# Three transposing loads for the first 512 rows of a cross network, in place of TensorE transposes

## The chip, the cores and the metric

The kernel runs on one core of one Trainium2 chip. The metric is device time in microseconds (us), the median of several runs. One execution is also taken with the hardware profiler; its span runs from the first instruction to the last. The engines are TensorE (PE; its weight loads are listed apart as PEld), VectorE (DVE), ScalarE (ACT), GpSimd (POOL) and SyncE (SP). DMAs are issued by SP and by ACT, each from its own queue of instructions.

## The reference

Six cross layers over 4096 rows of 416 features, in bf16. Each layer is a 416 x 416 matmul, a bias, a product with the input `x0`, and a sum with the layer's own input.

```python
B, F, D, L = 4096, 26, 16, 6
Din = min(F * D, 1024)          # 416
x0: (B, Din)   ws: (L, Din, Din)   bs: (L, Din)

def reference(x0, ws, bs):
    x = x0
    for l in range(ws.shape[0]):
        x = x0 * (x @ ws[l] + bs[l]) + x
    return x
```

## The kernel before

**The algebra.** Since `x` is always `x0` times something, the kernel never adds `x` back. It lets PSUM keep the sum of all layers' products: after layer l the banks hold the sum of `x_i @ W_i` for i up to l, and `x_{l+1} = x0 * (sum + summed biases + 1)`. The biases are summed once by a small matmul (`bias_sums`), with a row of ones for the 1.

**The tiling.** Rows are taken in 4 blocks of 1024 (`s`), each in two halves of 512 (`h`). The 416 features are 3 chunks of 128 (`c`, `m`, `k`) and a tail of 32. Activations are held transposed, features on partitions: `x0T_sb` has the 3 chunks of all rows, `xT_sb` the current layer's. The tail has its own layout: four groups of 256 rows are stacked on 128 partitions (`x0t_sb`, `xt_sb`), with a second copy in which neighbouring groups are swapped.

**One layer** (`s`, `l`) in the order in which TensorE gets it:

- `main` for half 0: 3 x 3 groups of four matmuls (128 rows of weights x 32 columns each, 512 moving columns), 36 in all;
- `tail_rows`: the tail's contribution to the chunks (needs `wt_sb`, the last 32 rows of the weights) and, in its second part, the tail's contribution to the tail (needs `wc_sb`, which POOL fills from `wt_sb` by four partition-shifting copies, `corner`);
- `tail_outs`: the chunks' contribution to the tail, for all 1024 rows, so it needs both halves;
- `main` for half 1, another 36 matmuls.

DVE takes each finished bank and multiplies by `x0T_sb` (`leave`, three for each half). ACT and POOL do the same for the tail (`leave_tail`): two ACT operations add the bias, POOL multiplies, and two copies each on ACT and POOL make the swapped copy. In the last layer of the last block the roles of the operands are turned, so that the output comes out by rows; it is not touched by the change.

**The head.** For the first 512 rows there is a special path. Two loads (`load_rows`, one on SP, one on ACT) bring them by rows into `xin_sb`. TensorE transposes them, 128 x 128 at a time, 12 in all, against the identity `ident`; DVE (chunks 0 and 2) and ACT (chunk 1) copy the results from PSUM to `x0T_sb`. Ahead of that TensorE runs 10 filler matmuls on a tile of ones, and 2 more between the two groups of transposes (`fill`). Rows 512 to 1023, and each later block, come by a transposing DMA (`load_transposed`). Layer 0 of block 0 has its own order: `main` goes chunk by chunk (`k` outermost), with `bias_sums` after chunk 0 and the tail's own transposes (`tail_in`, from `xin_sb` for rows 0 to 511 and `xtl_sb` for rows 512 to 1023) after chunk 1, then `tail_outs`, then `tail_rows`.

**What sets the order.** `Plan.add` records every operation by engine with what it reads and writes, and `emit` turns that into semaphore waits. Each engine works through its own list in the order in which the operations were added, and so do the two DMA-issuing queues. The order is thus that of the calls in the source: the loads (L208 to L225), the constants (L228 to L246), the head (L475 to L503), `corner` (L525, L526 and L558) and the loop (L527 on).

The loads, in the order of issue: SP has rows 0 to 255, W0, two of the four pieces of layer 0's tail weights (`wt0`), narrow rows (`xtl0`, 4 groups of 128 rows by 32 columns), the transposing load of rows 512 to 1023, four pieces of `wt1`, W1, four pieces of `wt2` (layers 2 to 5), W2, the other narrow rows, W3 to W5, and three transposing loads of 1024 rows. ACT has rows 256 to 511, the biases, and the other two pieces of `wt0`; its activation table is loaded behind these.

Of the kernel before, what the change touches and what calls it, by code (L numbers as in the profile page):

```python
# [5 lines left out]
BF16 = mybir.dt.bfloat16  # L6
FP32 = mybir.dt.float32
ALU = mybir.AluOpType
ACTF = mybir.ActivationFunctionType
# [109 lines left out]
def bass_standalone__dcn_v2_cross__recsys_kernel(  # L119
# [6 lines left out]
    B, D = x0.shape  # L126
# [15 lines left out]
    with ExitStack() as es:  # L142

        def sb(name, shape, dt=BF16):
            return es.enter_context(nc.sbuf_tensor(name, shape, dt))
# [1 line left out]
        w_sb = sb("w_sb", [128, L, NC, D])  # L147
        wt_sb = sb("wt_sb", [128, L, D])
        wc_sb = sb("wc_sb", [128, L, 2, 128])
        xin_sb = sb("xin_sb", [128, 4, D])  # L150
        xtl_sb = sb("xtl_sb", [128, NJ, DR])
        xr_sb = sb("xr_sb", [128, JS, D])
        x0T_sb = sb("x0T_sb", [128, NC, B])
# [9 lines left out]
        ot_sb = sb("ot_sb", [128, NS - 1, 2, 128])  # L163
        o_sb = sb("o_sb", [128, NJ, D])
        ident = sb("ident", [128, 128])
        ones_sb = sb("ones_sb", [128, 256])
        dummy_sb = sb("dummy_sb", [128, 8])
        bsa_sb = sb("bsa_sb", [L + 1, D])
        u_sb = sb("u_sb", [L + 1, L])
# [3 lines left out]

        x0_v = x0.rearrange("(j p) d -> p j d", p=128)
        out_v = out.rearrange("(j p) d -> p j d", p=128)
        P = Plan()

        def quad(q):
# [6 lines left out]
        def load(queue, dst, src, name, writes):  # L185
            P.add(queue, lambda e: e.dma_start(dst, src), writes=writes, dma=name)

        def load_main(l):
            load(
                "sync", w_sb[:, l, :, :], ws[l, 0:DF, :].rearrange("(k p) n -> p k n", p=128), "w%d" % l, [("w", l)]  # L190
            )

        def load_rows(queue, i):
            load(queue, xin_sb[:, 2 * i:2 * i + 2, :], x0_v[:, 2 * i:2 * i + 2, :], "xin%d" % i, [("xin", i)])

        def load_tail_weights(a, b, name, queues):
            for g in range(4):
# [1 line left out]
                    queues[g], wt_sb[quad(g), a:b, :], ws[a:b, DF:D, :].rearrange("l p n -> p l n"), name, [("wt", name)]  # L199
                )  # L200

        def load_transposed(s, a, b):
            P.add(
                "sync", lambda e: e.dma_start_transpose(x0T_sb[:, :, s * SB + a:s * SB + b], x0[s * SB + a:s * SB + b, 0:DF]),
                writes=[("x0T", s, c, h) for c in CH for h in HALVES if a <= h * H < b], dma="x0T%d" % s,
            )

        load_rows("sync", 0)  # L208
        load_rows("scalar", 1)
        load_main(0)  # L210
        load("scalar", bsa_sb[1:L + 1, :], bs[:, :], "bs", [("bs",)])
        load_tail_weights(0, 1, "wt0", ("sync", "scalar", "sync", "scalar"))
        load("sync", xtl_sb[:, 4:JS, :], x0_v[:, 4:JS, DF:D], "xtl0", [("xtl", 0)])
        load_transposed(0, H, SB)
        load_tail_weights(1, 2, "wt1", ("sync",) * 4)
        load_main(1)
        load_tail_weights(2, L, "wt2", ("sync",) * 4)
        load_main(2)
        load("sync", xtl_sb[:, JS:NJ, :], x0_v[:, JS:NJ, DF:D], "xtl1", [("xtl", 1)])
# [3 lines left out]
        for s in range(1, NS):  # L223
# [3 lines left out]

        P.add("vector", lambda e: e.memset(ones_sb[:, :], 1.0), writes=[("ones",)])  # L228
        P.add(
            "scalar", lambda e: e.activation(out=dummy_sb[:, :], in_=ones_sb[:, 0:8], func=ACTF.Identity, bias=0.0),  # L230
            reads=[("ones",)], writes=[("dummy",)],
        )
        P.add(
            "gpsimd", lambda e: e.affine_select(
# [29 lines left out]
        def fill(n):  # L264
            def fn(pe):
                for i in range(n):
                    ins = pe.matmul(  # L267
                        ps[:, 7, 0:256], lhsT=ones_sb[:, 0:128], rhs=ones_sb[:, :], start=True, stop=True
                    )
                return ins  # L270

            P.add("tensor", fn, reads=[("ones",)], adds=[("ps", 7)])

        def wkey(l):
            return "wt%d" % min(l, 2)
# [85 lines left out]
        def tail_in(s):  # L361
            def fn(pe):
                for o in range(2 if s == 0 else 1):
                    for r in range(2):
                        for g in range(4):
                            j = 2 * (g ^ o) + r
                            src = xin_sb[:, j, DF:D] if s == 0 and j < 4 else xtl_sb[:, s * JS + j, :]
                            b, c = (7, o * G) if s == 0 else (T_BANK[0], G)
                            ins = mm(
                                pe, ps[quad(g), b, c + r * 128:c + (r + 1) * 128], src, ident[:, :],  # L370
                                s == 0 and o == 0 and r == 0, (0, 32 * g),
                            )
                return ins

            b = 7 if s == 0 else T_BANK[0]
            P.add(
                "tensor", fn, reads=[("ident",), ("xtl", 0 if s == 0 else 1)] + ([("xin", 0), ("xin", 1)] if s == 0 else []),
                adds=[("ps", b)],
            )
            if s == 0:  # L380
                P.add(
                    "scalar", lambda e: e.activation(  # L382
                        out=x0t_sb[:, s, :, :], in_=ps[:, 7, :].rearrange("p (o c) -> p o c", o=2), func=ACTF.Copy
                    ), reads=[("ps", 7)], writes=[("x0t", s), ("x0t", s, "swapped")],
                )
# [83 lines left out]
                reads=[("o", s), ("oc", s)], writes=[("out", s)], dma="out%d" % s,  # L469
            )  # L470


        HEAD_BANKS = ((3, 4, 5), (6, 2, 7))
        B_BANK = 6
        fill(10)  # L475
        for i in range(2):
            for c in CH:
                b = HEAD_BANKS[i][c]

                def fn(pe, i=i, c=c, b=b):  # L480
                    for j in range(2):
                        ins = pe.transpose(  # L482
                            out=psT[:, b, j * 128:(j + 1) * 128],
                            in_=xin_sb[:, 2 * i + j, c * 128:(c + 1) * 128], identity=ident[:, :],
                        )
                    return ins

                P.add("tensor", fn, reads=[("xin", i), ("ident",)], adds=[("ps", b)])
                dst, src = x0T_sb[:, c, i * 256:(i + 1) * 256], psT[:, b, 0:256]
                if c == 1:  # L490
                    P.add(
                        "scalar", lambda e, d=dst, s=src: e.activation(out=d, in_=s, func=ACTF.Copy),
                        reads=[("ps", b)], writes=[("x0Tp", c, i)],
                    )
                else:
                    P.add(
                        "vector", lambda e, d=dst, s=src: e.tensor_copy(out=d, in_=s),  # L497
                        reads=[("ps", b)], writes=[("x0Tp", c, i)],
                    )
            if i == 0:  # L500
                fill(2)
        for c in CH:
            P.writer[("x0T", 0, c, 0)] = [w for i in range(2) for w in P.writer[("x0Tp", c, i)]]  # L503

        def bias_sums():
            def fn(pe):
# [16 lines left out]


        corner(0, 1, "wt0")  # L525
        corner(1, 2, "wt1")  # L526
        for s in range(NS):  # L527
            for l in range(L):
                ending = s == NS - 1 and l == L - 2
                if s == NS - 1 and l == L - 1:  # L530
                    break
                if s == 0 and l == 0:
                    for k in CH:
                        for m in CH:
                            main(s, l, 0, m, k)
                        if k == 0:
                            bias_sums()
                        if k == 1:
                            tail_in(0)
                    tail_outs(s, l, True)  # L540
                    tail_rows(s, l, False)
                    for c in CH:
                        leave(s, l, 0, c)
                else:
                    for m in CH:
                        for k in CH:
                            main(s, l, 0, m, k)
                    tail_rows(s, l, l == 0)
                    for c in CH:
                        leave(s, l, 0, c)  # L550
                    tail_outs(s, l, False)
                if l == 2 and s < NS - 1:
                    tail_in(s + 1)
                leave_tail(s, l, not ending)
                if l == 2 and s < NS - 1:
                    keep_tail_in(s + 1)
                if s == 0 and l == 0:
                    corner(2, L, "wt2")  # L558
                if l == 1 and s > 0:
                    store_block(s - 1)  # L560
                if s < NS - 1 and l in (3, 4):
                    g = 2 * (l - 3)
                    swap(x0t_sb[:, s + 1], ("x0t", s + 1), tuple("scalar" if q // 2 == l - 3 else None for q in range(4)))
                if ending:
                    tail_halves(L - 1, st_sb, ("st",))
                    for c in CH:
                        keep_sum(0, c, "scalar")
                for m in CH:
                    for k in CH:
                        main(s, l, 1, m, k)  # L570
                    leave(s, l, 1, m)
                if ending:
                    for c in CH:
                        keep_sum(1, c, ("scalar", "vector", "vector")[c])
            if s < NS - 1:
                transpose_block(s)
# [127 lines left out]
```

## Time and profile before

| | |
|---|---|
| median of 3 runs | 130.66 us (130.54 to 130.81) |
| the profiled execution | 130.68 us, span 129.4 us |
| PE busy | 124.5 us, 96% of the span |
| PEld busy | 64.3 us, 50% |
| DVE busy | 98.9 us, 76% |
| ACT busy | 50.5 us, 39% |
| POOL busy | 38.7 us, 30% |
| HBM read, written | 4.07 MB, 3.41 MB |

"Busy" adds up the time in which an engine has at least one instruction running; matmuls overlap each other, so a busy PE is not PE at its peak. The costliest group is line 259, the matmuls of `mm`, through which nearly all of them go. A row of the timeline reads: start in us from the start of the span, length in us, engine, line of the code, operation, tile written and tile read, shape, and count where neighbours are merged; in brackets the idle time of the engine ahead of it and what ended it. `SPq` and `ACTq` are DMA issues: their length is what the issue takes, not the transfer. The time from issue to landing is listed apart.

### The profile page before, as it was taken

What the parts mean: (1) busy time and instruction counts of PE and PEld (TensorE: products, weight loads), DVE (VectorE), ACT (ScalarE), POOL (GpSimd) and SP (SyncE); (2) the same over time, 40 slices, a digit from 0 to 9 for tenths busy, and PEclk for the clock granted to TensorE, in tenths of its full rate; (3) what the DMA queues carried; (4) which work ended last, traced back from release to release, by engine and by line L of the source; (5) the groups of instructions that cost most, each with busy time, mean ns of one, the idle gap of its engine ahead of it and who ended that gap; (6) DMA issues with size and microseconds to landing.
All of it is one profiled execution on the core that took longest, in us unless ns stands there. A gap on an engine that the chain in (4) does not pass through costs nothing.

```text
span 129.4 us, 5183 instructions
## 1 busy us (share of the span) xinstructions
PE 124.5 (96%) x2352; PEld 64.3 (50%) x2352; DVE 98.9 (76%) x151; ACT 50.5 (39%) x113; POOL 38.7 (30%) x86
## 2 busy tenths in 40 slices
PE   6999999999999999999999999999999999999990
PEld 4544545545545545545545545545545545544650
DVE  0309879779779779788788788798797797797881
ACT  1525225455505224464514233463513243245720
POOL 6044344044024053043123152142122152242050
PEclk9999999999999999999999999999999999999999
DMA  3989999999729307000019208000009507000007
GB/s 111 232 206 223 145 245 213 173 195 170 221 51 156 64 11 262 5 0 5 0 39 193 42 0 268 0 5 0 5 16 132 120 5 263 5 0 5 0 0 263
DMA packets 34065, 13.11 MB, mean 101 GB/s; under 512 B 25334, under 2 KB 34044, under 8 KB 34044
## 3 DMA queue, kind: packets, MB, share of 16 engines
q1 hardware_dynamic: 33248, 12.20, 45.2%
q10 hardware_dynamic: 796, 0.59, 1.4%
q8 instruction: 18, 0.29, 1.0%
q14 instruction: 3, 0.02, 0.1%
HBM read 4.07 MB, written 3.41 MB: 58 GB/s over the span
## 4 chain that ended last, share of the span: by engine, by line
PE 92%; DVE 2%; DMA 2%; ACT 0%; issue 0%
PE ps L259 91%; DVE o_sb L630 2%; DMA xin_sb<-in_x_dram 2%; PE ps L482 1%; ACT x0t_sb L382 0%; PE ps L267 0%
## 5 line engine op out<-in xcount | busy, mean ns | idle before, releaser
L411 DVE SCALAR_TENSOR_TENSOR xT_sb<-ps,cb_sb,x0T_sb 128x512 bf16<-128x512 f32 x120 | 80.9, 743 | 19.8 <-PE ps L259 19.8
L259 PE MATMUL ps<-xT_sb,w_sb 128*32 128x512 bf16 (+1 forms) x1596 | 84.6, 364 | 0.0
L259 PEld LDWEIGHTS ps<-xT_sb,w_sb 128*32 128x32 bf16 x1596 | 40.8, 97 | 37.2 <-issue 4.0
L421 ACT ACTIVATE t_sb<-ps,cb_sb 64x256 f32<-64x256 f32 x46 | 21.6, 470 | 51.1 <-PE ps L259 50.9
L434 POOL TENSOR_TENSOR xt_sb<-t_sb,x0t_sb 128x256 bf16<-128x256 f32 x20 | 13.4, 672 | 63.8 <-ACT t_sb L421 63.8
L398 ACT ACTIVATE xt_sb<-xt_sb 32x256 bf16<-32x256 bf16 x38 | 15.7, 414 | 15.4 <-POOL xt_sb L434 15.2
L259 PE MATMUL ps<-x0T_sb,w_sb 128*32 128x512 bf16 (+1 forms) x336 | 19.5, 373 | 0.1
L400 POOL COPY xt_sb<-xt_sb 32x256 bf16<-32x256 bf16 x38 | 15.0, 394 | 2.4
L411 DVE SCALAR_TENSOR_TENSOR xo_sb<-ps,cb_sb,x0T_sb 128x512 bf16<-128x512 f32 x18 | 12.1, 743 | 2.5 <-PE ps L259 2.5
L259 PEld LDWEIGHTS ps<-x0T_sb,w_sb 128*32 128x32 bf16 x336 | 8.4, 97 | 8.1 <-issue 0.8
L259 PE MATMUL ps<-xt_sb,wt_sb 32*128 32x512 bf16 (+1 forms) x152 | 11.6, 326 | 0.0
L259 PE MATMUL ps<-xt_sb,wc_sb 32*128 32x256 bf16 x76 | 7.3, 268 | 0.0
L259 PEld LDWEIGHTS ps<-xt_sb,wt_sb 32*128 32x128 bf16 x152 | 2.3, 91 | 8.1 <-DVE xT_sb L411 6.4
L259 PE MATMUL ps<-w_sb,xT_sb 128*128 128x416 bf16 x24 | 5.0, 339 | 0.0
L434 POOL TENSOR_TENSOR xot_sb<-t_sb,x0t_sb 128x256 bf16<-128x256 f32 x3 | 2.0, 674 | 9.9 <-ACT t_sb L421 9.9
L398 ACT ACTIVATE x0t_sb<-x0t_sb 32x256 bf16<-32x256 bf16 x12 | 4.9, 410 | 0.1
L252 POOL COPY wc_sb<-wt_sb 32x32 bf16<-32x32 bf16 (+1 forms) x12 | 2.8, 234 | 5.5 <-DMA wt_sb<-in_ws_dram 4.9
L267 PE MATMUL ps<-ones_sb 128*128 128x256 bf16 x12 | 2.9, 419 | 1.3 <-DVE ones_sb L228 1.3
L259 PEld LDWEIGHTS ps<-xt_sb,wc_sb 32*128 32x128 bf16 x76 | 3.9, 93 | 0.3
L497 DVE COPY x0T_sb<-ps 128x256 bf16<-128x256 bf16 x4 | 1.2, 292 | 3.6 <-PE ps L482 3.4
L630 DVE TENSOR_TENSOR o_sb<-ps,xr_sb 128x416 bf16<-128x416 f32 x6 | 3.1, 584 | 1.0 <-PE ps L259 1.0
L641 POOL TENSOR_TENSOR o_sb<-f_sb,xr_sb 128x416 bf16<-128x416 f32 x2 | 1.9, 976 | 4.8 <-ACT f_sb L637 4.8
(40 smaller groups left out, 34.5 us busy)
## 6 DMA issues: line engine op xcount, KB each, us to landing
out_dram<-o_sb SPq DMA_DIRECT2D x3, 832.0 KB, 4.2
w_sb<-in_ws_dram SPq DMA_DIRECT2D x6, 312.0 KB, 5.0
xr_sb<-in_x_dram SPq DMA_DIRECT2D x1, 832.0 KB, 5.8
wt_sb<-in_ws_dram SPq DMA_DIRECT2D x4, 104.0 KB, 3.1
out_dram<-o_sb SPq DMA_DIRECT2D x2, 208.0 KB, 2.2
xin_sb<-in_x_dram ACTq DMA_DIRECT2D x1, 208.0 KB, 3.2
xin_sb<-in_x_dram SPq DMA_DIRECT2D x1, 208.0 KB, 2.9
out_dram<-o_sb ACTq DMA_DIRECT2D x1, 208.0 KB, 2.4
```

What stands on the lines that cost most here:

```text
L252: "gpsimd", lambda e, p=p, g=g: e.tensor_copy(out=wc_sb[p, a:b, g % 2, quad(g)], in_=wt_sb[p, a:b, DF:D]), reads=[("wt", name), ("wc", nam ...
L259: return pe.matmul(dst, lhsT=lhsT, rhs=rhs, start=start, stop=True, skip_group_check=True, tile_position=pos,)
L267: ins = pe.matmul(ps[:, 7, 0:256], lhsT=ones_sb[:, 0:128], rhs=ones_sb[:, :], start=True, stop=True)
L398: fn = lambda e, d=dst, s=src: e.activation(out=d, in_=s, func=ACTF.Copy)
L400: fn = lambda e, d=dst, s=src: e.tensor_copy(out=d, in_=s)
L411: "vector", lambda e: e.scalar_tensor_tensor(out=dst, in0=ps[:, bank(h, c), :], scalar=cb_sb[:, c, l:l + 1], in1=x0T_sb[:, c, o:o + H], op ...
L421: "scalar", lambda e, p=p, h=h: e.activation(out=dst[p, :], in_=ps[p, T_BANK[h], 0:G], func=ACTF.Identity, bias=cb_sb[p, NC, l:l + 1]), re ...
L434: "gpsimd", lambda e: e.tensor_tensor(out=dst, in0=t, in1=x0t_sb[:, s, 0, :], op=ALU.mult),
L482: ins = pe.transpose(out=psT[:, b, j * 128:(j + 1) * 128], in_=xin_sb[:, 2 * i + j, c * 128:(c + 1) * 128], identity=ident[:, :],)
L497: "vector", lambda e, d=dst, s=src: e.tensor_copy(out=d, in_=s),
L630: "vector", lambda e: e.tensor_tensor(out=o_sb[:, jj, :], in0=ps[:, b, 0:D], in1=xr_sb[:, j, :], op=ALU.mult), reads=[("ps", b), ("xr",)], ...
L641: "gpsimd", lambda e: e.tensor_tensor(out=o_sb[:, jj, :], in0=t, in1=xr_sb[:, j, :], op=ALU.mult),
```

## The change

- The first 512 rows come by three transposing loads on SP, one for each chunk of 128 features, straight into `x0T_sb`. `xin_sb`, `load_rows`, the twelve TensorE transposes and the six copies from PSUM are gone, and so are the two fillers between them.
- W0 is the first load of the ACT queue, followed by the biases, the narrow rows (now 8 groups of 128 rows, since rows 0 to 511 no longer come by rows) and all four pieces of `wt0`. On SP the transposing load of rows 512 to 1023 follows the three new loads; then W1, ahead of `wt1`.
- Ahead of the first layer there are 15 fillers. They and ACT's first activation use a constant that the program's preamble sets up anyway; they no longer read the tile of ones, which shrinks to 128 columns.
- In layer 0 of block 0 `tail_rows` and the three `leave` come ahead of `tail_outs`. POOL's `corner` copies for layer 1 move from the head to the place behind layer 0's tail.

```diff
-        def load_main(l):
+        def load_main(l, queue="sync"):
...
-        def load_rows(queue, i):
-            load(queue, xin_sb[:, 2 * i:2 * i + 2, :], x0_v[:, 2 * i:2 * i + 2, :], "xin%d" % i, [("xin", i)])
...
-        def load_transposed(s, a, b):
-            P.add(
-                "sync", lambda e: e.dma_start_transpose(x0T_sb[:, :, s * SB + a:s * SB + b], x0[s * SB + a:s * SB + b, 0:DF]),
-                writes=[("x0T", s, c, h) for c in CH for h in HALVES if a <= h * H < b], dma="x0T%d" % s,
-            )
-
-        load_rows("sync", 0)
-        load_rows("scalar", 1)
-        load_main(0)
+        def load_transposed(s, a, b, chunks=slice(0, NC), name=None):
+            P.add(
+                "sync", lambda e: e.dma_start_transpose(
+                    x0T_sb[:, chunks, s * SB + a:s * SB + b],
+                    x0[s * SB + a:s * SB + b, 128 * chunks.start:128 * chunks.stop],
+                ),
+                writes=[
+                    ("x0T", s, c, h) for c in range(chunks.start, chunks.stop) for h in HALVES if a <= h * H < b
+                ], dma=name or "x0T%d" % s,
+            )
+
+        for c in CH:
+            load_transposed(0, 0, H, slice(c, c + 1), "x0T0_%d" % c)
+        load_main(0, "scalar")
         load("scalar", bsa_sb[1:L + 1, :], bs[:, :], "bs", [("bs",)])
-        load_tail_weights(0, 1, "wt0", ("sync", "scalar", "sync", "scalar"))
-        load("sync", xtl_sb[:, 4:JS, :], x0_v[:, 4:JS, DF:D], "xtl0", [("xtl", 0)])
+        load("scalar", xtl_sb[:, 0:JS, :], x0_v[:, 0:JS, DF:D], "xtl0", [("xtl", 0)])
+        load_tail_weights(0, 1, "wt0", ("scalar",) * 4)
         load_transposed(0, H, SB)
+        load_main(1)
         load_tail_weights(1, 2, "wt1", ("sync",) * 4)
-        load_main(1)
         load_tail_weights(2, L, "wt2", ("sync",) * 4)
...
-                        ps[:, 7, 0:256], lhsT=ones_sb[:, 0:128], rhs=ones_sb[:, :], start=True, stop=True
+                        ps[:, 7, 0:256], lhsT=const[:, 0:128], rhs=const, start=True, stop=True
...
-                            src = xin_sb[:, j, DF:D] if s == 0 and j < 4 else xtl_sb[:, s * JS + j, :]
+                            src = xtl_sb[:, s * JS + j, :]
...
-        HEAD_BANKS = ((3, 4, 5), (6, 2, 7))
         B_BANK = 6
-        fill(10)
-        for i in range(2):
-            for c in CH:
...
-                P.add("tensor", fn, reads=[("xin", i), ("ident",)], adds=[("ps", b)])
...
+        fill(15)
...
         corner(0, 1, "wt0")
-        corner(1, 2, "wt1")
...
-                    tail_outs(s, l, True)
-                    tail_rows(s, l, False)
+                    tail_rows(s, l, True)
                     for c in CH:
                         leave(s, l, 0, c)
+                    tail_outs(s, l, False)
...
                 if s == 0 and l == 0:
+                    corner(1, 2, "wt1")
                     corner(2, L, "wt2")
```

More of the change, by code (lines that the diff above doesn't have):

```diff
@@ L149, in bass_standalone__dcn_v2_cross__recsys_kernel @@
         wc_sb = sb("wc_sb", [128, L, 2, 128])
-        xin_sb = sb("xin_sb", [128, 4, D])
         xtl_sb = sb("xtl_sb", [128, NJ, DR])
@@ L165, in bass_standalone__dcn_v2_cross__recsys_kernel @@
         ident = sb("ident", [128, 128])
-        ones_sb = sb("ones_sb", [128, 256])
+        ones_sb = sb("ones_sb", [128, 128])
         dummy_sb = sb("dummy_sb", [128, 8])
@@ L175, in bass_standalone__dcn_v2_cross__recsys_kernel @@
         out_v = out.rearrange("(j p) d -> p j d", p=128)
+        const = nc.const_aps.tensor(1.0, [128, 256], BF16)
         P = Plan()
@@ L186, in load @@
             P.add(queue, lambda e: e.dma_start(dst, src), writes=writes, dma=name)
-        def load_main(l):
+        def load_main(l, queue="sync"):
             load(
-                "sync", w_sb[:, l, :, :], ws[l, 0:DF, :].rearrange("(k p) n -> p k n", p=128), "w%d" % l, [("w", l)]
+                queue, w_sb[:, l, :, :], ws[l, 0:DF, :].rearrange("(k p) n -> p k n", p=128), "w%d" % l, [("w", l)]
             )
-        def load_rows(queue, i):
-            load(queue, xin_sb[:, 2 * i:2 * i + 2, :], x0_v[:, 2 * i:2 * i + 2, :], "xin%d" % i, [("xin", i)])
         def load_tail_weights(a, b, name, queues):
@@ L229, in bass_standalone__dcn_v2_cross__recsys_kernel @@
         P.add(
-            "scalar", lambda e: e.activation(out=dummy_sb[:, :], in_=ones_sb[:, 0:8], func=ACTF.Identity, bias=0.0),
-            reads=[("ones",)], writes=[("dummy",)],
+            "scalar", lambda e: e.activation(out=dummy_sb[:, :], in_=const[:, 0:8], func=ACTF.Identity, bias=0.0),
+            writes=[("dummy",)],
         )
@@ L267, in fn @@
                     ins = pe.matmul(
-                        ps[:, 7, 0:256], lhsT=ones_sb[:, 0:128], rhs=ones_sb[:, :], start=True, stop=True
+                        ps[:, 7, 0:256], lhsT=const[:, 0:128], rhs=const, start=True, stop=True
                     )
                 return ins
-            P.add("tensor", fn, reads=[("ones",)], adds=[("ps", 7)])
+            P.add("tensor", fn, adds=[("ps", 7)])
         def wkey(l):
@@ L376, in tail_in @@
             P.add(
-                "tensor", fn, reads=[("ident",), ("xtl", 0 if s == 0 else 1)] + ([("xin", 0), ("xin", 1)] if s == 0 else []),
+                "tensor", fn, reads=[("ident",), ("xtl", 0 if s == 0 else 1)],
                 adds=[("ps", b)],
@@ L470, in store_block @@
             )
-        HEAD_BANKS = ((3, 4, 5), (6, 2, 7))
         B_BANK = 6
-        fill(10)
-        for i in range(2):
-            for c in CH:
[L478 to L484, printed above, removed]
-                        )
-                    return ins
-                P.add("tensor", fn, reads=[("xin", i), ("ident",)], adds=[("ps", b)])
-                dst, src = x0T_sb[:, c, i * 256:(i + 1) * 256], psT[:, b, 0:256]
-                if c == 1:
-                    P.add(
[L492 to L503, printed above, removed]
+        fill(15)
         def bias_sums():
```

## The prediction

> **What bounds the kernel now.** I read the chain that ended last first, then the same chain in order of time, then the first 16 us instruction by instruction, then the landing times of the loads. The page's chain, by engine and by line:
>
> ```profile
> PE 92%; DVE 2%; DMA 2%; ACT 0%; issue 0%
> ```
>
> and in order of time (start, length, what ran):
>
> ```profile
> 0.81 2.93 DMA xin_sb<-in_x_dram
> ...
> 3.79 0.82 PE ps L482 x6
> 4.61 0.43 PE ps L267 x2
> 5.03 0.64 PE ps L482 x6
> 5.67 2.64 PE ps L259 x49
> ...
> 8.34 0.61 ACT x0t_sb L382
> ...
> 8.99 114.53 PE ps L259 x2139
> ```
>
> From 8.99 us TensorE never waits again until 123.5. The page has no other engine above 76% of the span, so what follows 8.99 moves as a block: the change is worth as many microseconds as it brings this block forward, or loses by pushing it back. I therefore cost only the head, and take as its mark the start of the second half of the first layer, the 36 matmuls at 9.98, because everything behind them runs without a gap. The head in the timeline (start, length, engine, line, operation):
>
> ```profile
> 1.26 2.31 PE L267 MATMUL ps<-ones_sb 128*128 128x256 bf16 x10 [1.26 <-DVE ones_sb L228]
> 3.28 1.81 SPq L204 DMA_TRANSPOSE x0T_sb<-in_x_dram  x1
> 5.63 1.47 PE L259 MATMUL ps<-x0T_sb,w_sb 128*32 128x512 bf16 x12
> 6.96 1.01 POOL L252 COPY wc_sb<-wt_sb 32x32 bf16<-32x32 bf16 x4 [3.56 <-DMA wt_sb<-in_ws_dram]
> 7.23 0.83 PE L259 MATMUL ps<-x0T_sb,w_sb 128*32 128x512 bf16 x12
> 8.34 0.60 ACT L382 ACTIVATE x0t_sb<-ps 128x512 bf16<-128x512 f32 x1 [0.77 <-PE ps L259]
> 9.43 0.60 PE L259 MATMUL ps<-x0t_sb,wt_sb 32*128 32x512 bf16 x7
> 9.98 2.13 PE L259 MATMUL ps<-x0T_sb,w_sb 128*32 128x512 bf16 x36
> 66.20 1.25 SPq L451 DMA_TRANSPOSE o_sb<-xo_sb  x1
> 70.24 1.24 SPq L456 DMA_TRANSPOSE ot_sb<-xot_sb  x1
> ```
>
> The same twelve matmuls take 1.47 us at 5.63 and 0.83 at 7.23: TensorE ran at about half speed until some 7.0 us, 5.8 us after its first filler. Less the end of the pipeline (0.2 us), twelve cost 1.28 us slow and 0.65 fast. The rows by DMA issue give the landings (count, KB, us from issue to landing):
>
> ```profile
> x0T_sb<-in_x_dram SPq DMA_TRANSPOSE x1, 4.6
> ot_sb<-xot_sb SPq DMA_TRANSPOSE x1, 2.3
> o_sb<-xo_sb SPq DMA_TRANSPOSE x1, 3.2
> w_sb<-in_ws_dram SPq DMA_DIRECT2D x1, 312.0 KB, 3.7
> ```
>
> They are, in order, the load of rows 512 to 1023 issued at 3.28, the tail transpose at 70.24, the chunk transpose at 66.20, and W0.
>
> **Removed.** Two row loads, twelve TensorE transposes, two fillers between them (0.82 + 0.43 + 0.64 = 1.9 us on the chain) and six copies from PSUM. The copies end at 6.0; DVE is idle until 9.90 anyway, so they cost only what TensorE waits for the first one. The shorter memset of ones is worth nothing: ident, which it feeds, is next needed by the tail transposes at 7.9.
>
> **Fillers.** They wait for no memset now, so they start with the first DMA issues, near 0.85 instead of 1.26. Ten take 2.31 with a tail of 0.2, so 0.21 each; fifteen end at 0.85 + 3.15 + 0.2 = 4.2. That hides behind the loads unless these land before 4.2.
>
> **First chunk and W0.** No row shows a transposing load of 512 x 128 from memory. Landing: from below the 2.3 us of the 128 x 256 tail transpose, from above the 3.2 us of the 128 x 1024 chunk transpose: 3.1 to 4.0. W0 leaves first on ACT at 0.80; with 3.2 us (208 KB of rows on that queue, the page's row) to 3.7 us it lands at 4.0 to 4.5. I take 4.25 for the first matmul, against 5.63.
>
> **Issue of a chunk load on SP.** 1024 blocks of 256 bytes took 1.25 us at 66.20 and the 1536 of the load at 3.28 took 1.81: a slope gives about 0.67 for 512. Above stands the 1.24 of the tail transpose, with only 256 blocks, which says that there may be a floor; below, a third of 1.81, 0.60. That tail transpose followed three others without a gap and so may have been held up by them, while the chunk transpose started on an empty queue; so I take 0.67. With 0.05 between issues SP is at the second-half load (rows 512 to 1023) at 0.81 + 3 x 0.72 = 2.97, and it lands 4.6 later, at 7.6; with 1.25 each, at 0.81 + 3.9 + 4.6 = 9.3. The other end of that bound is 0.81 + 3 x 0.65 + 4.6 = 7.4.
>
> **Layer 0 on TensorE.** The clock: with the same 5.8 us after the first filler it rises at 6.65. Chunk 0 from 4.25 to 5.53 slow; bias sums 0.2; chunk 1 from 5.73, nine matmuls slow and three fast, to 6.8 (chunk 1 issued at 1.53 has 4.2 us to land, chunk 2 at 2.25 has over 4.8). Then the tail transposes at 6.8: they need the 64 KB of narrow rows, issued on ACT at 2.0 after W0 (0.48) and the biases (0.65), landing 4.3 later by the 32 KB row, 6.3. From tail transposes at 7.89 to TensorE's release at 8.99 it took 1.10, through the ACT copy (chunk 2's matmuls lie under it): release at 7.9. All clock slow would make this 8.07; fast from the start, 7.4 (bounded by 6.3 + 1.1).
>
> **Tail weights, now all on ACT.** After the narrow rows (0.43 for 32 KB, 1.41 for 192 KB: 0.63 for 64) the four issue at 2.63 to 4.3, 0.42 each. The last, issued at 3.9, lands 2.1 to 3.7 later by the rows of such 26 KB loads: 6.0 to 7.6, I take 6.6. POOL's four copies take 1.01: 7.6 (7.0 to 8.6). ACT's table load, 1.28, moves behind these issues to 4.3 to 5.6, hidden, since its first real work comes near 5.8.
>
> **The reordered end of layer 0.** Tail rows, 0.55 (9.43 to 9.98), now start at max(7.9, 7.6) = 7.9 and end at 8.45. Then the tail outputs, 0.44 (8.99 to 9.43), which need both halves (7.6): 8.9. The second half's matmuls start at 8.9 instead of 9.98. **Gain 1.1 us.** All slow gives 0.9, fast from the start 7.6 + 0.55 + 0.44 = 8.6, so 1.4.
>
> **What is late next.** POOL now does layer 1's corner copies behind layer 0's tail product and swaps. From the end of the tail outputs: two ACT halves to 1.1, product 0.67 and swaps 0.85 with gaps to 2.8, corners to 3.85. Layer 1's second tail matmuls are due after two sets of 36 (2.05 each) and the first tail set, at 4.3: 0.4 spare, provided the wt1 loads, now behind w1 on SP (issued 5.3 to 7.2), have landed by 11.7, and 3.1 us put them at 10.3. SP's other loads: w2 leaves at 9.15 against 9.58 before, so nothing downstream is later; with 1.25 per chunk load it leaves at 10.9 and lands 4.7 later at 15.6, while its matmuls are due a layer (4.88) after 11.93 less the gain, 15.7.
>
> [...]
>
> **Sum.** The profiled execution took 130.68 (span 129.4 and 1.3 around it), as good as the 130.66 median. 130.68 - 1.1 = **129.6**.
>
> **Rivals.** (1) *The chunk loads cost an issue floor.* At 1.25 each the second half lands at 9.3, TensorE waits for it ahead of the tail outputs, the mark is 9.74: 130.4; where the 4.6 shrinks because nothing else is ahead of it in the queue, down to 129.8. For it: 1.24 us for 256 blocks. (2) *The slower side: the issue cost goes by the 512 rows*, so each chunk load takes the full 1.81. SP reaches the second half at 0.81 + 3 x 1.86 = 6.39, landing at 11.0, mark 11.44: 132.1. It decides from a landing at 9.54, that is from 1.38 per load. Against it: 1.25 for eight column blocks. (3) *ACT's issues stand behind SP's transposes.* The tail weights would be issued from 4.8 to 6.5, the last landing near 8.8; corners at 9.8, second half at 10.8: 131.5. Against it: both queues' loads at 0.80 and 0.81 took 0.48 and 0.46, no stretch; no row has ACT issuing under a transpose. [...] (4) *The gain is eaten later*: wt1 lands after 12.1, layer 1 waits, and the time stays at 130.5.
>
> **Chances.** Forecast 0.55, alone 129.2 to 130.1; rival 1 0.19 (0.13 of it clear of no change); rival 2 0.11; rival 3 0.09; rival 4 0.06. About 0.2%, 0.26 us, is what can be told from no change: faster 0.55 + 0.13 = 0.68, same 0.06 + 0.06 = 0.12, slower 0.11 + 0.09 = 0.20. The range 128.9 to 131.0 takes in the fast clock with early corner copies, and rival 1 whole; it leaves out rivals 2 and 3.
>
> **What would show it.** Right: three SP transposes near 0.7 us each from 0.81; first main matmuls near 4.25; the ACT copy of x0t ending near 7.9; DVE's first product near 8.4 instead of 9.90; 36 matmuls near 8.9; no new wait in layers 1 and 2. Wrong: SP issues of 1.2 us and more; TensorE idle ahead of the tail outputs for x0T; corner copies starting after 7.5; ACT issues much longer than 0.45.

## The result, and the profile after

The changed kernel takes 131.59 us (median of 20 runs, 130.50 to 132.63) against 130.28 for the kernel before (20 runs, 129.71 to 130.81): a ratio of 1.0088, 95% interval 1.0069 to 1.0107. It is slower by 0.9%, where 129.6 was forecast. (The ratio leaves out the two longest of the 20 runs, 132.52 and 132.63, as slow ones, so it is not the quotient of the two medians.) The profiled execution took 131.81 us with a span of 130.6, against 130.68 and 129.4.

The chain that ended last, in order of time (start, length, what ran), of the changed kernel. Line numbers are those of the changed kernel, in which matmuls are line 261 and the transposing loads line 201:

```profile
0.80 1.21 SPq L201
2.02 0.06 issue
2.08 4.94 DMA x0T_sb<-in_x_dram
7.01 0.04 issue
7.06 117.62 PE ps L261 x2169
```

The old chain reached TensorE's unbroken block over a load of rows, two sets of transposes and half a layer. This one consists of two things: SP needs 1.21 us to issue the first chunk load, and the second one, issued at 2.08, lands only at 7.02. The block itself is of the same kind as before, but its beginning is not, as the timeline of TensorE shows (start, length, operation, in brackets the idle time ahead and what ended it):

```profile
0.84 3.12 PE L269 MATMUL ps<-const-bfloat16-1.0 128*128 128x256 bf16 x15 [0.84 <-PEq L661]
...
5.64 0.83 PE L261 MATMUL ps<-x0T_sb,w_sb 128*32 128x512 bf16 x12 [1.68 <-DMA x0T_sb<-in_x_dram]
...
7.06 1.47 PE L261 MATMUL ps<-x0T_sb,w_sb 128*32 128x512 bf16 x12 [0.40 <-DMA x0T_sb<-in_x_dram]
...
8.31 0.65 PE L261 MATMUL ps<-ident,xtl_sb 128*32 128x128 bf16 x16
...
8.73 1.50 PE L261 MATMUL ps<-x0T_sb,w_sb 128*32 128x512 bf16 x12
```

The three rows of twelve matmuls are chunks 0, 1 and 2 of the same layer. Chunk 0 takes 0.83 us, chunks 1 and 2 1.47 and 1.50: TensorE had reached its full speed and lost it again. The windows of the trace show when. Columns: stretch, its length, busy time of PE, PEld, DVE, ACT and POOL with counts, the granted clock, share of the DMA engines, GB/s:

```profile
0.17:3.58 3.41, 2.74 (x14) 1.91 (x15) 0.17 (x1) 0.00 (x0) 2.33 (x8) 1.00 0.43 106
3.58:6.99 3.41, 1.40 (x31) 0.53 (x29) 0.00 (x0) 1.68 (x3) 0.00 (x0) 1.00 1.26 164
6.99:10.40 3.41, 3.34 (x46) 1.40 (x50) 0.00 (x0) 0.60 (x1) 0.82 (x4) 0.50 1.05 241
10.40:13.80 3.40, 3.40 (x76) 1.86 (x72) 3.07 (x5) 1.62 (x4) 1.27 (x3) 1.00 0.88 212
```

The clock changed at 3.57, 6.99 and 10.40, that is in steps of 3.41 us (ahead of the first change the column reads 1.00, though the fillers there run slow: 0.42 us for one, and 0.27 for the last, at 3.69). After a stretch with TensorE busy for 2.74 us it rose; after one with 1.40 us it fell; after one with 3.34 it rose. In e5 (below) TensorE was busy for 2.85 us between 11.99 and 15.40, and the clock rose only at 18.81. What decides it is not shown. The 1.68 us of waiting for chunk 0 and 0.40 for chunk 1 lie in the second.

The landings, as rows of the DMA view (count, us from issue to landing), for chunks 0, 1 and 2 and the second half's load, in this order:

```profile
x0T_sb<-in_x_dram SPq DMA_TRANSPOSE x1, 4.7
x0T_sb<-in_x_dram SPq DMA_TRANSPOSE x1, 4.9
x0T_sb<-in_x_dram SPq DMA_TRANSPOSE x1, 4.8
x0T_sb<-in_x_dram SPq DMA_TRANSPOSE x1, 4.5
```

Chunk 0 is there at 5.5, chunk 1 at 7.0, chunk 2 at 8.1, the second half at 9.2. W0 had landed at 4.1.

**Where the time can go.** The prediction held that everything behind the head moves as a block. The start of layer 1's first matmuls is a mark for that: 11.93 before, 13.09 after, 1.16 later, and the profiled executions differ by 131.81 - 130.68 = 1.13. So the whole loss lies ahead of 13.09 us. The table below holds to this in every experiment within 0.05 us.

### The profile page after: what moved, and what is told of

It reads as the page before. It is cut to its first block, busy times and chain, and to the rows that moved or that the text cites. A ratio compares the mean times of both kernels' runs of the same rounds, so it can differ in the third digit from the quotient of the medians.

```text
span 130.6 us, 5158 instructions
## 1 busy us (share of the span) xinstructions
PE 124.3 (95%) x2343; PEld 64.0 (49%) x2343; DVE 97.6 (75%) x147; ACT 49.7 (38%) x111; POOL 38.5 (29%) x86
## 3 DMA queue, kind: packets, MB, share of 16 engines
HBM read 3.68 MB, written 3.41 MB: 54 GB/s over the span
## 4 chain that ended last, share of the span: by engine, by line
PE 90%; DMA 4%; DVE 2%; SPq 1%; issue 0%
PE ps L261 90%; DMA x0T_sb<-in_x_dram 4%; DVE o_sb L602 2%; SPq L201 1%
## 5 line engine op out<-in xcount | busy, mean ns | idle before, releaser
L261 PE MATMUL ps<-x0T_sb,w_sb 128*32 128x512 bf16 (+1 forms) x336 | 20.0, 382 | 2.1 <-DMA x0T_sb<-in_x_dram 2.1
L269 PE MATMUL ps<-const-bfloat16-1.0 128*128 128x256 bf16 x15 | 3.1, 393 | 0.8 <-PEq L661 0.8
```

What stands on the lines that cost most here:

```text
L261: return pe.matmul(dst, lhsT=lhsT, rhs=rhs, start=start, stop=True, skip_group_check=True, tile_position=pos,)
L269: ins = pe.matmul(ps[:, 7, 0:256], lhsT=const[:, 0:128], rhs=const, start=True, stop=True)
```

## The experiments

| kernel | median, us | ratio to before (95%) | its profiled execution, us | layer 1 starts, us |
|---|---|---|---|---|
| before | 130.28 | | 130.68 | 11.93 |
| changed | 131.59 | 1.0088 (1.0069 to 1.0107) | 131.81 | 13.09 |
| e1 fillers for the gaps | 130.85 | 1.0041 (1.0020 to 1.0062) | 130.91 | 12.15 |
| e2 one load for three | 131.83 | 1.0103 (1.0073 to 1.0133) | 131.84 | 13.12 |
| e3 chunk 0 alone | 134.85, one execution | | 134.85 | 16.09 |
| e4 old order | 131.44 | 1.0079 (1.0051 to 1.0106) | 132.65 | 13.88 |
| e5 W0 beside chunk 0 | 138.12, one execution | | 138.12 | 19.39 |
| e6 64-byte rows last | 131.24 | 1.0062 (1.0039 to 1.0086) | 131.42 | 12.66 |
| e8 before, constant fillers | 130.04 | 0.9985 (0.9965 to 1.0004) | 130.61 | 11.86 |
| e9 W0 first on SP | 131.43 | 1.0057 (1.0024 to 1.0091) | 130.68 | 11.95 |
| e10 the same, fillers | 130.80 | 1.0033 (1.0012 to 1.0054) | 130.73 | 12.00 |
| e11 before, no fillers | 130.87 | 1.0037 (1.0006 to 1.0067) | 130.99 | 12.23 |
| e12 one load, fillers | 131.33 | 1.0077 (1.0054 to 1.0101) | 131.34 | 12.58 |
| e13 as e8 | 130.14 | 1.0006 (0.9984 to 1.0028) | 130.14 | 11.38 |
| e14 W0 first on SP, 20 fillers | 130.87 | 1.0048 (1.0023 to 1.0074) | 130.98 | 12.22 |

Each ratio is to runs of the kernel before on the same chip. (e7 was the first try of e12; see the last section.)

**Theories.** "Landing": the chunk loads land too late because other loads are in flight beside them. "Clock": the waiting that this opens lets the clock fall. Rivals: the order at the end of layer 0; an issue floor for each load; the small rows; the choice of queue.

### Is it the clock? (e1)

```diff
-        fill(15)
+        fill(24)
...
                         if k == 0:
                             bias_sums()
+                            fill(4)
```

> The changed kernel with 24 fillers instead of 15 and four more behind the bias sums, so that TensorE has work until chunk 0 lands (5.51 us) and again until chunk 1 lands (7.02). Theory 'clock': in the changed kernel the clock falls to 0.5 from 6.99 to 10.4 because TensorE idled 1.7 us; kept busy it stays at 1.00, chunks 1 and 2 take 0.65 us each instead of 1.28, the second half's matmuls start near 10.1 instead of 11.2, and the time falls from 131.6 to about 130.5. Rival 'landing alone': the late landings cost by themselves and the clock has no share: 131.6, within 0.3.

130.85, ratio 1.0041. One row from each of the two kernels' windows, from 5 to 10 us; first the changed kernel:

```profile
5.00:10.00 5.00, 3.96 (x68) 1.65 (x68) 0.00 (x0) 2.02 (x4) 0.82 (x4) 0.70 1.15 213
```

and e1:

```profile
5.00:10.00 5.00, 4.94 (x98) 2.41 (x99) 0.21 (x1) 2.02 (x4) 0.82 (x4) 1.00 1.11 220
```

TensorE is kept busy (4.94 us), the clock rises once, at 6.11, and stays (the column reads 1.00 ahead of that too), and with the loads landing about as late as before (5.4, 6.9 and 8.0) the time falls by 1.0088 - 1.0041 = 0.0047, some 0.6 us; the two intervals do not overlap. The rival, that the landings alone cost, is out. Whether the clock is the only cause e1 cannot say: 0.5 us remain against the kernel before, but no load stands in e1's chain, and its own fillers do:

```profile
0.84 5.28 PE ps L269 x24
6.12 0.96 PE ps L261 x24
7.08 0.55 PE ps L269 x4
```

I expected 130.5: the 24 fillers ended only at 6.1 in the profiled execution, after chunk 0 had landed, and the four take 0.55 us of the chain while chunk 1, there since 6.9, waits.

### What makes the chunks land late? (e3, e5, e6, e9)

e3 holds all of ACT's loads until chunk 0 has landed (the first line changed below; `load` and `load_main` pass on a list of what is read); e5 lets W0 go at once and holds the rest (the second).

```diff
-        load_main(0, "scalar")
+        load_main(0, "scalar", [("x0T", 0, 0, 0)])
...
-        load("scalar", bsa_sb[1:L + 1, :], bs[:, :], "bs", [("bs",)])
+        load("scalar", bsa_sb[1:L + 1, :], bs[:, :], "bs", [("bs",)], [("x0T", 0, 0, 0)])
```

The expectations of e3 and of e5:

> The changed kernel in which ACT's first load waits until chunk 0 has landed, so nothing else is in flight beside it but chunks 1 and 2 on its own queue. Theory 'neighbours': W0 and the 64-byte rows beside it make chunk 0 land 4.7 us after its issue; alone it lands after about 3.2 us, as the transposes from SBUF do (at 4.0). Rival 'intrinsic': a transposing load of 512 x 128 from memory takes about 4.7 us by itself, so it lands at 5.5 again. The time of the whole is longer under both, by 2 us or more, since W0 comes later.

> The changed kernel in which ACT issues W0 at once and holds everything behind it (biases, 64-byte rows, tail weights) until chunk 0 has landed. In the changed kernel chunk 0 landed 4.7 us after its issue, alone 2.8. Theory 'small rows': the 1024 pieces of 64 bytes are what holds its completion up; with W0 alone beside it chunk 0 lands 2.8 to 3.3 us after issue, by 4.1. Rival 'W0's bytes': sharing the DMA engines with 312 KB is what costs, and it lands at 4.5 us or more after issue, 5.3 or later.

Chunks 0, 1 and 2 of e3 (us from issue to landing):

```profile
x0T_sb<-in_x_dram SPq DMA_TRANSPOSE x1, 2.8
x0T_sb<-in_x_dram SPq DMA_TRANSPOSE x1, 2.7
x0T_sb<-in_x_dram SPq DMA_TRANSPOSE x1, 4.8
```

and of e5:

```profile
x0T_sb<-in_x_dram SPq DMA_TRANSPOSE x1, 4.4
x0T_sb<-in_x_dram SPq DMA_TRANSPOSE x1, 3.8
x0T_sb<-in_x_dram SPq DMA_TRANSPOSE x1, 2.9
```

In e3 chunks 0 and 1 travel alone and land in 2.8 and 2.7; chunk 2 meets W0, which ACT issued at 3.60, and needs 4.8. In e5 it is the other way round: chunk 0 beside W0 takes 4.4, chunk 2, with W0 down at 4.0 and the rest held back, takes 2.9. The same load, 128 KB, takes 2.8 us or 4.8 us according to what flies beside it. By these single executions W0 accounts for 1.6 of the 1.9 us that chunk 0 is late; my expectation that the 64-byte rows were to blame fell. For chunks 1 and 2 the smaller loads do matter: 3.8 and 2.9 in e5 against 4.9 and 4.8 in the changed kernel.

e6 puts the 64-byte rows behind the tail weights on ACT:

```diff
-        load("scalar", xtl_sb[:, 0:JS, :], x0_v[:, 0:JS, DF:D], "xtl0", [("xtl", 0)])
         load_tail_weights(0, 1, "wt0", ("scalar",) * 4)
+        load("scalar", xtl_sb[:, 0:JS, :], x0_v[:, 0:JS, DF:D], "xtl0", [("xtl", 0)])
```

> The changed kernel with the 64-byte rows last on ACT, behind the four tail weight loads. Theory 'small rows': chunks 0 and 1 land sooner, near 4.2 and 5.5, and TensorE starts before the clock can fall; but the tail transposes then wait for rows that land near 8, so the time falls by 0.5 us at most, to 131.1 to 131.6. Rival 'W0's bytes': chunk 0 again at 5.4 or later, time 131.6 or more.

131.24, 1.0062; its interval overlaps that of the changed kernel. Chunk 0 landed at 5.4 again, chunk 2 at 7.9: the rows' place is not the cause.

e9 takes W0 off ACT's queue and puts it ahead of the chunks on SP's:

```diff
+        load_main(0)
         for c in CH:
             load_transposed(0, 0, H, slice(c, c + 1), "x0T0_%d" % c)
-        load_main(0, "scalar")
```

> The changed kernel with W0 as SP's first load, ahead of the three chunk loads, and off ACT's queue, where biases, 64-byte rows and tail weights now come first. Theory 'neighbours on the other queue': chunk 0 alone landed 2.8 us after issue, beside W0 4.4, in the changed kernel 4.7; behind W0 on the same queue and beside ACT's small loads chunk 0 (issued at 1.3) lands near 4.6 to 5.0, chunk 2 near 6.3 to 6.8, the tail weights by 6.5; TensorE starts near 4.7, the second half's matmuls near 9.2 to 10.0, time 129.6 to 130.4. Rival 'bytes': the queue makes no difference, chunk 0 lands at 5.5 or later and the time is 131.5 or more.

131.43, 1.0057. Chunk 0, now behind W0, took 4.5 us from its issue at 1.33 and landed at 5.9, chunk 2 at 8.3. For chunk 0 the queue makes no difference that these executions show, 4.4 us beside W0 on the other queue (e5) and 4.5 behind it on its own (e9); W0's company does, against 2.8 without it (e3). The profiled execution of e9 is no slower than the profiled one of before (130.68); in it the clock rose at 4.7 and stayed; the runs as a whole spread from 130.18 to 132.78.

### What is left with the clock up? (e10, e14, e2, e12)

e10 is e9 with more fillers; e14 has the 20 and not the four behind the bias sums.

```diff
-        fill(15)
+        fill(20)
...
                             bias_sums()
+                            fill(4)
```

The expectations of e10 and of e14:

> The same with 20 fillers and four more behind the bias sums. Theory 'clock': where TensorE idles less than in the changed kernel the fillers bring less, 0 to 0.5 us: 129.4 to 130.2. Rival: fillers that run at the slow clock delay chunk 0, and it is 0.3 us slower than without them.

> W0 first on SP and 20 fillers, without the four behind the bias sums. Theory 'landing': with the clock up what is left is the last chunk's landing, 8.0 to 8.3 (5.9 us was when the copies of the third chunk began in the kernel before), so tail rows start near 9.1 and the kernel comes no lower than before: 130.3 to 130.7, ratio 1.000 to 1.003. Rival 'it was only the clock and the fillers': 129.9 or less.

130.80 and 130.87, 1.0033 and 1.0048, both above what I expected. The spread of e10 closes to 0.6 us (130.54 to 131.11) from the 2.6 of e9, which fits the clock: two of e9's runs have a mean granted clock of 0.985 and 0.986, e10's all have 0.998 or more. The floor does not come down, but the four fillers take 0.55 us of e10's chain too. e14 has none there; its chain, behind the issue of W0:

```profile
1.31 1.19 SPq L201
2.49 0.05 issue
2.55 5.04 DMA x0T_sb<-in_x_dram
7.58 0.04 issue
7.63 116.18 PE ps L261 x2179
```

With the clock up from 6.11, TensorE stood idle for 0.72 us until chunk 1 landed at 7.58; the tail rows began at 9.39 and layer 1 at 12.22. The order of bounds that I expected was off by one chunk, but the rival (129.9 or less) is out: the late landings cost by themselves.

e2 has one load of 512 x 384; e12 has it together with e1's fillers.

```diff
-        for c in CH:
-            load_transposed(0, 0, H, slice(c, c + 1), "x0T0_%d" % c)
+        load_transposed(0, 0, H, name="x0T0_a")
```

The expectations of e2 and of e12:

> The changed kernel with one transposing load of 512 x 384 in place of the three chunk loads. Theory 'floor per load': three issues of 1.21 to 1.25 us and a landing of 4.7 to 4.9 us each are what makes chunk 2 land at 8.13; one load takes 1.8 us to issue and lands at 0.81 + 4.6 = 5.4 to 6.0, the second half's load at 7.3 to 8.0; tail transposes near 7.2, second half's matmuls near 9.5 to 10.3, time 129.8 to 130.9. Rival 'the landing goes by bytes and neighbours': the one load lands no earlier than chunk 2 did, near 8: time 131.5 or more, as TensorE starts later and the clock falls.

> The one-load kernel with 24 and 4 fillers again, since its first profile has the clock at half speed for all of its 255 us. Theory 'clock': with the clock up by 6.5 the profile shows chunks in 0.65 us each and 131.0 or less. Rival: 131.6 as its other three runs, with TensorE waiting for a load (tail rows, tail weights) rather than for the clock.

One load took 1.34 us to issue in e2 and landed at 6.0 with all three chunks, two microseconds ahead of the third chunk load. The time did not fall (131.83): TensorE's first matmul moved to 6.13, and in the profiled execution the clock fell at 7.63. With fillers it is 131.33, where I expected 131.0 or less, and its interval overlaps that of e2. The chain of e12 names what is late next:

```profile
4.25 4.60 DMA wt_sb<-in_ws_dram
8.85 0.05 issue
8.90 0.21 POOL wc_sb L253
...
9.97 114.20 PE ps L260 x2135
```

The tail weights, last on ACT's queue, land at 8.85, and POOL's four copies end at 9.9. Before the change the same copies began at 6.96.

### The other parts (e4, e8, e13, e11)

e4 restores the old order of layer 0's end and the place of the corner copies.

```diff
-                    tail_rows(s, l, True)
+                    tail_outs(s, l, True)
+                    tail_rows(s, l, False)
                     for c in CH:
                         leave(s, l, 0, c)
-                    tail_outs(s, l, False)
...
         corner(0, 1, "wt0")
+        corner(1, 2, "wt1")
```

> The changed kernel with the old order at the end of layer 0 (tail outputs ahead of tail rows and the three products) and layer 1's corner copies back in the head. Theory 'clock and landing': the order is worth nothing here, since the second half of the rows has landed (9.16) before TensorE gets to either part (10.17): 131.6, within 0.3. Rival 'order': the moved corner copies or the earlier products cost or save 0.5 us or more.

131.44, 1.0079 (1.0051 to 1.0106): the same as the changed kernel. The order is worth nothing that this measurement, good to some 0.3%, can tell.

e8 and e13 are the kernel before with its fillers on the constant.

```diff
+        const = nc.const_aps.tensor(1.0, [128, 256], BF16)
...
-                        ps[:, 7, 0:256], lhsT=ones_sb[:, 0:128], rhs=ones_sb[:, :], start=True, stop=True
+                        ps[:, 7, 0:256], lhsT=const[:, 0:128], rhs=const, start=True, stop=True
...
-            P.add("tensor", fn, reads=[("ones",)], adds=[("ps", 7)])
+            P.add("tensor", fn, adds=[("ps", 7)])
...
-        fill(10)
+        fill(12)
```

The expectations of e8 and of e13:

> The kernel before with one part of the change alone: fillers on the constant, 12 instead of 10, starting at 0.85 instead of 1.26 and ending at the same time. Theory 'clock': the clock rises earlier in some executions, so the twelve matmuls of chunk 0 and part of chunk 1 run fast: 0.2 to 0.6 us faster than before, 129.7 to 130.1. Rival: the clock rises at the same time and nothing is gained, ratio within 0.2%.

> The kernel before with 12 fillers on the constant, measured again, since the first comparison (0.9985, 0.9965 to 1.0004) left open whether this part of the change is a gain by itself. Theory 'clock': an earlier start of the fillers lets the clock rise earlier in some executions, ratio 0.997 to 0.999. Rival: no difference, ratio within 0.001 of 1.

0.9985 (0.9965 to 1.0004) and 1.0006 (0.9984 to 1.0028). Starting the fillers 0.4 us sooner brings nothing that two measurements could tell. In the profiled execution of e13 the clock rose at 3.82, layer 1 began at 11.38, and that run took 130.14; in e8's it rose at 6.78, layer 1 began at 11.86, and that run took 130.61. Which it is varies from execution to execution.

e11 is the kernel before without any filler.

> The kernel before without any filler matmuls; nothing else is changed. Measures the price of a late clock by itself: TensorE starts at 3.8 instead of 1.3, so the clock rises one window (3.4 us) later in most executions, and some 2 to 3 us of matmuls run at half speed for longer: theory 'clock' expects 1.0 to 1.8 us more than before, 131.3 to 132.2. Rival 'the head is bound by loads, the clock matters little': within 0.4 us of before.

130.87, 1.0037: 0.5 us, half of the least that I expected; the interval (1.0006 to 1.0067) does not tell it from the rival's 0.4. In its profile the transposes began at 3.67 and the clock rose at 8.19. That is only 1.1 us later than the 7.12 in the profile of before, where I had counted on a full step of 3.4.

No version beat the kernel before.

## Why the prediction was wrong

**The step that failed** is the landing of the first chunk, "from below the 2.3 us ..., from above the 3.2 us", and with it that of chunks 1 and 2. Both rows came from transposes late in the kernel, with no load in flight beside them, while the load I priced leaves together with W0, and six more loads follow on ACT. As a price for a load that flies alone the bounds were right: e3 measured 2.8. As a price in its place they were not: 4.7 to 4.9. The row that would have told was on the page: the load at 3.28, in company, took 4.6, and I read that as the price of its size. Chunk 2 was late by a second term as well: it left at 3.36 and not at 2.25, since each issue took 1.2 us and not 0.67.

**What follows from it.** TensorE's first matmuls come at 5.64 instead of 4.25, and chunk 2, to which I gave "over 4.8" of slack from 2.25, lands at 8.1. TensorE runs dry twice (1.68 and 0.40 us), and this opens the second failure: I let the clock rise once and stay. It rose sooner than I took (3.57 for 6.65), and fell at 6.99, after 3.41 us in which TensorE was busy for 1.40. No term of my sum had this price. By e1 the clock, falls and late rises together, is about 0.6 of the loss of 1.15 us (0.88% of 130.28).

**Point by point.**
- *Fillers.* From 0.84 to 3.96; I had 0.85 to 4.2. Right, and without worth by themselves (e8, e13).
- *W0.* Landed at 4.14, within 4.0 to 4.5.
- *Issue on SP.* 1.21 to 1.25 us for each load, at the upper bound of 0.60 to 1.25, where I took 0.67. The tail transpose's 1.24 for 256 blocks was the better witness: 512 x 384 took 1.34 when nothing stood ahead (e2), 0.13 more than the first chunk's 1.21 for a third of it. (The 1.38 per load at which rival 2 was to decide has the 0.05 between issues in it; without it is 1.33.)
- *Tail weights.* Landed at 8.4, not 6.6; the four issues took 2.33 us, not 1.68, under SP's transposes. The copies began at 8.42 and ended 9.42, outside my 8.6. Not the bound in the changed kernel, but the next one (e12).
- *Narrow rows.* Landed at 6.96, not 6.3; TensorE came to their transposes at 8.31.
- *Second half's load.* 9.2, near the upper bound of 9.3, and hidden: TensorE came to it at 10.80.
- *Order and corner copies.* Costed at nothing, worth nothing (e4); layer 1's tail matmuls followed its 36 without a wait.
- *The block behind.* Right in all kernels of the table.
- *Rivals.* The first (an issue floor) named the true issue cost, but priced it through the second half's load and came to 130.4; what it delayed was chunk 2. The third had ACT's issues queue behind SP's; they were stretched by 0.65 us, but went out from 2.37 to 4.70, under SP's from 0.80 to 6.36. That its 131.5 is next to the measured 131.59 is luck: it had the tail weights as the bound, and in the changed kernel they were not.
- *DMA against TensorE.* One load brought all twelve blocks of 128 x 128 in 5.2 us (e2). TensorE was the better place for them here all the same: no kernel with the chunks by DMA beat 130.28.

**What stays open.** The split of the other half, some 0.5 us, between the chunks' landings, the tail weights and e1's own fillers: the profiles name now the one and now the other (e1, e10, e12, e14), and no run tells them apart. What makes the clock rise or fall, beyond the steps of 3.41 us, is open too.

## What to carry to other kernels

Take the time to landing of a moved load from a row that had as much company as it will have, not from one that flew alone: here it was 2.8 us or 4.8. A wait ahead of a busy TensorE can cost twice: here 1.68 and 0.40 us for themselves, and twelve matmuls in 1.47 us in place of 0.83 at the clock that had fallen by then. So a plan for the head has to look at where TensorE waits, not only at the sum. Taking work off an engine that had the time for it gains nothing if its replacement stands in line for the resource that bounds the stage, here the loads of the first 8 us.

## What the runs showed that I had not expected

Executions of one kernel differ by where the clock's steps fall. Of the changed kernel's 20 runs the six with a mean granted clock of 0.984 to 0.987 took 131.68 to 131.94 us (one step of 3.41 us at half clock, in a span of 130.6, makes a mean of 0.987). The three shortest, 130.50 to 130.77, have 1.000, but so have the two longest, 132.52 and 132.63. The mean counts the time ahead of the first rise as 1.00, so a late rise does not show in it. The profiled execution of e4 is such a one: mean 1.000, but 132.65 us, and in it chunks 0 and 1 both ran slow.

```profile
5.67 1.47 PE L261 MATMUL ps<-x0T_sb,w_sb 128*32 128x512 bf16 x12 [1.46 <-DMA x0T_sb<-in_x_dram]
7.27 1.47 PE L261 MATMUL ps<-x0T_sb,w_sb 128*32 128x512 bf16 x12
```

There the clock rose only at 11.80. So the fall that the changed kernel's profile shows is, by their means, that of six runs in 20; e4's profile has a wait of 1.46 us there, no fall and a late rise. Whether that is what happened in the two longest runs is not shown, since they have no trace.

In e7, the first measurement of the one-load kernel with fillers, one execution took 256.44 us.

> One transposing load in place of three (it landed at 6.0) together with 24 fillers and four more behind the bias sums. Theory 'clock': the one-load kernel at 131.83 had its clock at 0.5 from 7.64 to 11.05; kept busy it stays at 1.00 and the time falls by 1 us, to 130.8, about the time of the three loads with the same fillers (130.85), since the tail weights land at 8.9 under both. Rival: no change, 131.8.

Its other three runs took 131.45 to 131.67, ratio 1.0087 (1.0054 to 1.0119). In the long one TensorE was busy from end to end at half its pace (784 matmuls in the 80 us from 80 to 160, against 412 in 20 us of the changed kernel), with no change of the clock on record. (e10's profile has none on record either, and ran at full pace, so an empty record decides nothing.) It did not come back in e12's ten runs; its cause is open.
